# Softcap attention and a maxout layer on one core: the handwritten order of the work rearranged from the second pair of heads to about the tenth quad

## The chip, the cores and the metric

The kernel runs on one core of a Trainium2 chip. The core has four engines that compute, each with its own queue of instructions: TensorE (PE in the profile, with its weight loads as PEld) multiplies matrices into PSUM, VectorE (DVE) works element by element, ScalarE (ACT) evaluates functions, and GpSimd (POOL) here mostly issues loads. SyncE (SP) issues the other transfers and passes on some waits. The metric is the device time of one execution in microseconds (us), as the median of several runs.

## The reference

Attention with a soft cap over 8 batches, 12 heads, 448 tokens and 64 columns a head; its output, 3,584 rows of 768, goes through a maxout layer of width 1,024. Inputs and output are float32.

```python
scores = scale * np.matmul(q, k.transpose(0, 1, 3, 2))      # scale = 1/sqrt(64)
scores = cap * np.tanh(scores / cap)                         # cap = 30
attn = np.exp(scores - max); attn = attn / (sum(attn) + 1e-09)
x = np.matmul(attn, v)           # heads side by side: 3584 x 768
h1 = x @ w1; h2 = x @ w2         # 768 x 1024
out = np.maximum(h1, h2) @ w_out # 1024 x 768
```

## The kernel before, in words

**What is computed.** max(x w1, x w2) w_out is written as relu(x wd) w_out + x wm, with wd = w1 - w2 and wm = w2 w_out. Both are made in the kernel at its start (steps W and WC turn w2 around, P with OP and PC multiply it by w_out, `sub` subtracts). Work is in bf16, sums in float32. Softmax takes no maximum, since tanh bounds the scores.

**How it is tiled.** Two heads are a pair (i = 0 to 47), two pairs a quad (t = 0 to 23). For each pair, TensorE makes scores transposed (keys on the partitions) in three blocks of 128 keys, steps `S i 0` to `S i 2`; the last 64 keys of a quad's four heads are one more block, step `L t`, the left scores. ACT takes each block through tanh (`T i j`, and `TL t`) and then exp over one to three blocks (`E i j0 j1`, `EL t`). DVE adds the blocks up (`A`, `B`; from quad 3 on), TensorE totals them (`Y t`), DVE inverts the totals (`Y1`, `Y2`, `Y3`), TensorE multiplies with the values (`VL t`, `V t u j0 j1`), and DVE normalizes (`N t 0` one instruction, L613; `N t 1` two, L616) into xT, the transposed x.

The maxout layer is 120 groups, 15 on average a batch: a group is one PSUM bank of 128 rows, summed over 6 blocks (448 columns, relu(x wd), kept transposed as gT) or over 14 blocks (384 columns, half an output tile: 6 of x wm and 8 of gT w_out). `O g bank` opens it. `M x y n` makes n steps in which the upper 64 rows of the array work for group x and the lower 64 for group y, side by side; x = y uses all 128 rows. So a group's two halves are made one after the other, by different rows of the array, into one bank. Between the halves stands a hand-over, `H g` on DVE or `Hs g` on SyncE: an instruction that computes nothing, waits for the last matmul of one half, and is waited for by the first of the other (L647 to L650). `ev g` takes a finished group out of PSUM on DVE (L661 with relu, L697 as a copy), `eva g` on ACT (L695).

**PSUM.** Two score slots s0 and s1 of two banks each are shared by S, L and the values: block j of pair i takes the slot `TURN[o*3+j] ^ (t%2)` with TURN = (0,1,0,1,1,0) and o the pair's place in the quad. The left scores take the slot that `s_tile(1, t)` names, the values that of `s_tile(0, t+1)`. So the third scores of the second pair of a quad, `S i 2` with odd i, take the slot that the values of the quad before were in, and cannot begin before that quad's normalize is done. Four banks mm0 to mm3 serve all else: groups, totals, transposes, premultiplication.

**Loads and turns.** GpSimd's queue loads q, k (lq, lk) and v (lv) with a cast to bf16, and the weights (lw1, lw2, lwo). The first five quads are turned by TensorE (X, copied by DVE with XC); from quad 5 on SyncE's queue issues a transposing transfer (`cr t`, L470), which waits for that quad's loads. SyncE also issues the output's stores (st).

**What sets the order.** One long text, ORDER, lines 9 to 195, names every step in turn, and a loop at the end runs it through a table of steps. The schedule is manual: on each engine the instructions stand in the order of the text, and waits come from the data, the buffers and the hand-overs alone. `D bank n` are dummy matmuls near the start. The changed text is found by step names; the profile shows lines:

- L411 W, L426 P, L432 PC, L453 X, L458 XC, L466 D
- L509 S, L514 T, L523 L, L527 TL, L531 E, L534 EL, L543 A, L548 B
- L561, L565, L568 Y, L573 Y1, L576 Y2, L579 Y3, L595 VL, L601 V, L613 and L616 N
- L640 M by halves, L635 M by whole rows, L661, L695, L697 evacuations

Of the kernel before, what the change touches and what calls it, by code (L numbers as in the profile page):

```python
# [14 lines left out]
OP 2 0 3; P 2 0 7; P 1 0 1; P 2 0 1; P 1 0 1; P 3 0 2; P 1 0 2; PC 2 0; PC 1 0; E 1 2 3; E 1 0 2; TL 1; T 2 0; EL 0;
S 3 0; S 2 2; P 3 0 1; W 0 2; P 3 0 1; X 4 3; T 2 2; T 3 0; VL 0; Y 0 1; V 0 0 0 3; V 0 1 0 3; S 3 1; lwo 1 0;
lwo 1 1; lq 5 0; lk 5 0; lv 1 0; lv 1 1; lk 8 0; lq 8 0; lq 7 0; lw2 4; lv 6 2; lq 6 0; lk 7 0; lk 6 0; lw2 5; lw1 2;
lw1 4; lw1 0; lv 2 0; lv 2 1; WC 0; PC 3 0; XC 4; Y1 0; Y2 0; Y3 0; N 0 0; N 0 1; E 2 0 3; T 3 1; EL 1; E 3 0 2;
OP 0 0 1; P 0 0 2; OP 2 1 2; P 2 1 2; P 0 0 1; OP 1 1 3; P 1 1 2; P 0 0 1; P 1 1 2; P 0 0 1; P 1 1 4; S 4 0; S 3 2;
X 5 0; P 2 1 4; P 0 0 3; P 2 1 1; XC 5; PC 1 1; PC 0 0; T 3 2; T 4 0; E 3 2 3; OP 3 1 3; P 3 1 1; P 2 1 1; S 4 1;  # L20
S 4 2; Y 1 1; T 4 1; T 4 2; L 2; P 3 1 4; VL 1; TL 2; V 1 1 0 3; V 1 0 0 3; S 5 0; X 6 0; E 4 0 3; T 5 0; EL 2; Y1 1;
Y2 1; PC 2 1; Y3 1; N 1 1; N 1 0; XC 6; X 7 2; W 4 1; S 5 2; S 5 1; X 8 0; P 3 1 3; WC 4; XC 8; PC 3 1; T 5 1; T 5 2;
OP 4 0 1; P 4 0 2; OP 0 1 0; P 0 1 3; S 6 0; S 6 1; W 5 3; P 0 1 1; P 4 0 6; P 0 1 4; E 5 0 2; T 6 1; T 6 0; E 5 2 3;
XC 7; sub 2 0; WC 5; sub 4 0; PC 4 0; sub 0 0; PC 0 1; OP 5 1 3; P 5 1 4; S 6 2; L 3; Y 2 1; T 6 2; TL 3; E 6 0 3;
VL 2; V 2 1 0 1; V 2 0 0 3; V 2 1 1 3; S 7 0; P 5 1 4; OP 5 0 0; P 5 0 8; Y1 2; Y2 2; Y3 2; N 2 0; N 2 1; A 3 0 1;
A 3 0 2; PC 5 1; PC 5 0; T 7 0; EL 3; lk 9 0; lq 11 0; lv 3 1; lq 9 0; lw1 1; lw1 3; lq 10 0; lk 12 1; lv 3 0; lw1 5;
lk 10 0; lk 11 0; lk 11 1; lk 10 1; S 7 2; O 0 1; M 0 -1 2; S 7 1; M 0 -1 4; O 1 2; M 1 -1 1; T 7 2; T 7 1; Hs 0;
M 1 -1 1; S 8 1; M 1 -1 1; M 1 0 3; S 8 0; X 9 3; OP 4 1 0; P 4 1 4; sub 1 0; sub 3 0; XC 9; T 8 1; E 7 0 2; T 8 0;
E 7 2 3; P 4 1 4; L 4; O 2 3; M 2 0 3; S 8 2; M 2 1 3; A 3 1 1; B 3 1; PC 4 1; ev 0; B 3 0; Hs 2; TL 4; T 8 2; O 3 0;
# [12 lines left out]
VL 5; A 5 1 2; TL 6; V 5 0 0 2; V 5 1 0 2; Y 5 3; E 12 0 3; V 5 0 2 3; V 5 1 2 3; Y1 5; S 13 0; M 13 11 1; lv 7 0;
M 13 11 1; Y2 5; M 13 12 2; Y3 5; M 13 12 1; lv 7 1; M 13 12 3; N 5 0; M 13 12 1; lv 7 2; M 13 12 1; T 13 0;
M 13 12 1; N 5 1; M 13 12 1; lv 7 3; M 13 12 1; O 14 3; M 14 12 2; EL 6; Hs 13; S 13 1; lk 18 0; M 14 12 1;
M 14 13 1; ev 11; M 14 13 1; Hs 12 2; T 13 1; S 13 2; lk 18 1; M 14 13 1; A 6 0 1; M 12 13 2; T 13 2; Hs 14;
M 12 13 1; lq 18 0; A 6 0 2; S 14 0; M 12 13 3; E 13 0 2; M 12 13 1; S 14 1; lk 19 0; M 12 13 1; O 15 0; M 15 13 2;
ev 12; M 15 13 1; lk 19 1; M 15 14 2; ev 13; M 15 14 1; T 14 0; O 16 1; M 16 14 1; lq 19 0; A 6 1 1; M 16 14 1;
st 0 1; M 16 14 1; Hs 15; T 14 1; cr 8; B 6 0; M 16 15 1; S 14 2; M 16 15 1; ev 14; M 16 15 1; T 14 2; O 17 2;
M 17 15 2; H 16; M 17 15 1; B 6 1; M 17 16 2; E 13 2 3; M 17 16 1; ev 15; O 18 3; M 18 16 1; L 7; VL 6; A 6 1 2;
st 0 2; TL 7; V 6 0 0 2; V 6 1 0 2; Y 6 0; E 14 0 3; V 6 0 2 3; V 6 1 2 3; Y1 6; S 15 0; M 18 16 1; lv 8 0;  # L50
M 18 16 1; Y2 6; M 18 17 1; Y3 6; M 18 17 1; lv 8 1; M 18 17 1; O 19 0; M 19 17 2; ev 16; Hs 18; lv 8 2; M 19 17 1;
M 19 18 1; T 15 0; N 6 0; M 19 18 2; lv 8 3; O 20 1; M 20 18 2; EL 7; Hs 19; ev 17; M 20 18 1; lk 20 0; S 15 1;
M 20 19 1; N 6 1; M 20 19 1; T 15 1; M 20 19 1; lk 20 1; O 21 2; M 21 19 3; Hs 20; M 21 20 1; lq 20 0; ev 18;
# [147 lines left out]
def kernel(  # L201
# [17 lines left out]
    B, H, S, D = q.shape  # L219
# [554 lines left out]
```

## Time and profile before

| | before |
|---|---|
| runs | 328.42, 327.58, 328.32 us; median 328.32 |
| profiled execution | 328.19 us, span 326.4 us |
| TensorE busy | 319.9 us, 98% of the span |
| ScalarE busy | 281.0 us, 86% |
| VectorE busy | 240.2 us, 74% |
| GpSimd busy | 161.8 us, 50% |
| TensorE's granted clock | 1.00 |
| moved by DMA | 46.28 MB, mean 142 GB/s |

The profiled execution is one run: its time contains its span and 1.8 us around it. A row of the timeline gives start and length, engine, line, operation, output and inputs, and how many instructions it groups; brackets at its end hold the engine's idle time before it and what ended that. A row of a grouping gives the count, the busy time, the mean in ns, and idle time before with what released it. TensorE's ends are modelled, so two of its rows may overlap, and the distance of two starts says more than a length.

### The profile page before, as it was taken

Reading aid. Unit: us, or ns where it says so; the run is one execution under the profiler, and the core shown is the slowest. Engines: PE = TensorE matmul, PEld = TensorE weight load, DVE = VectorE, ACT = ScalarE, POOL = GpSimd, SP = SyncE. Lnnn points to the kernel's source line nnn. Section 1 sums busy time; section 2 is a strip of 40 time slices with the busy share of each in tenths; the row PEclk is TensorE's granted clock in tenths of the full one; section 3 lists DMA queues with packets and bytes.
Section 4 is the critical chain, followed back from the end, with each engine's and each line's share of the span. In section 5 each row is a group of like instructions: output and inputs, shape, how many; then the busy total and the mean of one; then the engine's idle time right before and its main releaser. Section 6 shows DMA issues by size and latency. Waiting matters only on the chain.

```text
span 326.4 us, 9772 instructions
## 1 busy us (share of the span) xinstructions
PE 319.9 (98%) x4138; PEld 183.6 (56%) x4138; DVE 240.2 (74%) x422; ACT 281.0 (86%) x278; POOL 161.8 (50%) x237
## 2 busy tenths in 40 slices
PE   7999999999999999999999999999999999999994
PEld 3454545545656664565565565556466555557662
DVE  3346899987897778987897788968878779773201
ACT  5999999999999999999999999999999999921120
POOL 7357583677764682665775475578538311000000
PEclk9999999999999999999999999999999999999999
DMA  8999999899999999999999999999999963013033
GB/s 181 180 201 178 273 252 115 95 141 140 189 183 109 142 189 184 97 89 181 167 181 113 202 106 189 121 166 163 184 109 90 212 157 44 2 50 98 0 98 96
DMA packets 134507, 46.28 MB, mean 142 GB/s; under 512 B 112320, under 2 KB 129472, under 8 KB 134464
## 3 DMA queue, kind: packets, MB, share of 16 engines
q0 software_dynamic: 94592, 25.02, 77.6%
q1 hardware_dynamic: 39424, 19.99, 29.9%
q8 instruction: 32, 0.52, 0.7%
q10 hardware_dynamic: 448, 0.66, 0.6%
q14 instruction: 11, 0.09, 0.1%
HBM read 47.78 MB, written 11.01 MB: 180 GB/s over the span
## 4 chain that ended last, share of the span: by engine, by line
PE 94%; DMA 2%; DVE 1%; POOL 1%; issue 0%
PE mm L640 61%; PE s L509 9%; PE s L601 9%; PE mm L426 5%; DMA w2b<-in_moe_w_dram 2%; PE s L523 2%; PE mm L568 2%; PE s L595 2%; PE mm L635 1%; POOL kqs L316 1%; PE mm L453 1%; PE mm L411 1%; PE mm L561 1%; DVE xT L616 0%; PE mm L466 0%; DVE xT L613 0%
## 5 line engine op out<-in xcount | busy, mean ns | idle before, releaser
L514 ACT ACTIVATE e<-s 128x896 bf16<-128x896 f32 x144 | 125.7, 926 | 5.5 <-PE s L509 5.0
L531 ACT ACTIVATE e<-e 128x1792 bf16<-128x1792 bf16 (+2 forms) x72 | 122.8, 1708 | 0.0
L640 PE MATMUL mm<-wo_sb,gT 64*128 64x384 bf16 x864 | 115.2, 323 | 0.0
L640 PE MATMUL mm<-wm_sb,xT 64*128 64x384 bf16 x648 | 102.1, 322 | 0.0
L640 PE MATMUL mm<-xT,wd_sb 64*128 64x448 bf16 x768 | 97.6, 349 | 0.0
L323 POOL DMA_DIRECT2D kqs<-in_k_dram x76 | 54.6, 720 | 55.1 <-DMA qkT<-kqs 50.9
L640 PEld LDWEIGHTS <-gT 64*128 64x128 bf16 x864 | 58.6, 94 | 25.6 <-issue 1.1
L640 PEld LDWEIGHTS <-wd_sb 64*128 64x128 bf16 x768 | 48.3, 94 | 27.1 <-issue 2.1
L640 PEld LDWEIGHTS <-xT 64*128 64x128 bf16 x648 | 50.1, 94 | 18.5 <-issue 0.2
L509 PE MATMUL s<-qkT 64*128 64x448 bf16 x288 | 52.5, 352 | 0.2 <-DVE xT L613 0.2
L347 POOL DMA_DIRECT2D vp<-in_v_dram x48 | 30.4, 637 | 37.4 <-PE s L509 25.4
L661 DVE TENSOR_SCALAR gT<-mm 128x448 bf16<-128x448 f32 x64 | 39.0, 618 | 8.4 <-PE mm L640 7.6
L323 POOL DMA_DIRECT2D kqs<-in_q_dram x38 | 35.0, 922 | 3.9 <-issue 1.8
L601 PE MATMUL s<-e,vp 128*32 128x448 bf16 x576 | 36.1, 354 | 0.0
L543 DVE TENSOR_TENSOR esum<-e 128x896 bf16<-128x896 bf16 x42 | 25.9, 618 | 9.1 <-ACT e L531 9.1
L616 DVE TENSOR_TENSOR xT<-s,inv 64x448 bf16<-64x448 f32 x48 | 29.8, 622 | 1.7 <-PE s L601 0.8
L543 DVE TENSOR_TENSOR esum<-esum,e 128x896 bf16<-128x896 bf16 x42 | 26.2, 624 | 5.9 <-ACT e L531 4.8
L509 PEld LDWEIGHTS <-qkT 64*128 64x128 bf16 x288 | 18.7, 94 | 20.1 <-issue 11.3
L695 ACT COPY osb<-mm 128x384 f32<-128x384 f32 x10 | 4.8, 479 | 26.9 <-PE mm L640 26.7
L697 DVE COPY osb<-mm 128x384 f32<-128x384 f32 x44 | 23.3, 554 | 6.2 <-PE mm L640 5.7
L548 DVE TENSOR_TENSOR esum<-esum,el 64x896 bf16<-64x896 bf16 x42 | 26.0, 619 | 1.2
L573 DVE STREAM_TRANSPOSE st<-mm 128x448 f32<-128x448 f32 x24 | 15.6, 649 | 12.9 <-PE mm L568 11.3
(57 smaller groups left out, 269.9 us busy)
## 6 DMA issues: line engine op xcount, KB each, us to landing
out_dram<-osb SPq DMA_DIRECT2D x54, 192.0 KB, 4.8
vp<-in_v_dram POOLq DMA_DIRECT2D x38, 160.0 KB, 3.9
kqs<-in_q_dram POOLq DMA_DIRECT2D x46, 112.0 KB, 5.3
kqs<-in_k_dram POOLq DMA_DIRECT2D x76, 56.0 KB, 3.9
osb<-in_moe_w_dram POOLq DMA_DIRECT2D x4, 512.0 KB, 6.9
w2b<-in_moe_w_dram POOLq DMA_DIRECT2D x6, 256.0 KB, 7.7
wo_sb<-in_moe_w_out_dram POOLq DMA_DIRECT2D x4, 384.0 KB, 9.9
vp<-in_v_dram POOLq DMA_DIRECT2D x10, 128.0 KB, 7.8
```

The costliest lines, as they stand in the source:

```text
L323: nc.gpsimd.dma_start(out=to, in_=x)
L347: nc.gpsimd.dma_start(out=to, in_=x)
L509: scored[i, j] = nc.tensor.matmul(s[:, h, :S], k_of(t, o, h, j), q_of(t, o, h)).ins
L514: nc.scalar.activation(expo[i][:, 2 * j : 2 * j + 2, :], slots[i, j][:, :, :S], AF.Tanh, scale=scale / cap)
L531: nc.scalar.activation(e, e, AF.Exp, scale=float(cap))
L543: nc.vector.tensor_add(d, e[:, 0:2, :] if j == 1 else d, e[:, 2 * j : 2 * j + 2, :])
L548: nc.vector.tensor_add(d, d, left_e[t][r, :, :])
L601: nc.tensor.matmul(vals[t][place(m, u), u, :S], w[:, m, :], expo[2 * t + o][:, 2 * j + h, :], start=False, stop=(j == NJ - 1))
L616: nc.vector.tensor_mul(x[64 - r : 128 - r], vals[t][r : r + 64, u, :S], sums[t, 3][64 - r : 128 - r])
L640: ins = nc.tensor.matmul(self.ps, w[r], x[r], start=first, stop=self.at == [self.n, self.n]).ins
L661: nc.vector.tensor_relu(gT[b // 2][:, f, cs], ps)
L697: nc.vector.tensor_copy(o[:, hs], ps)
```

## The change

ORDER is another text from the second pair on. Each kind of step occurs as often as before. Loads, DMA issues and hand-overs are also at other places of the text, but the order on each queue is what counts:

- GpSimd's queue: no difference.
- TensorE: another order from about 12.6 us of the profile before to the step S 20 2, which begins at 122.39; all later steps are in the same order.
- ACT: another order from quad 1 to E 19 2 3 (pair 19). The evacuations of groups 24, 27 and 29 move from DVE to ACT.
- DVE: another order up to about quad 10.
- SyncE: another order up to about the transfer of quad 13.
- Hand-overs on DVE 31 in place of 21, on SyncE 103 in place of 107; the groups 1, 10, 12, 17, 24 and 27 have one at a place where there was none.
- Some steps use another of the four banks (W, X, Y, P, and groups 26 and 27).

One line of code differs, in the transposes: the bank is taken when one is named, and not when the part is other than 1. For the steps of this text the two give the same. The text is five lines longer, so L640 of before is L645 of after.

```diff
-T 1 0; T 1 2; lw2 1; lwo 0 0; lwo 0 1; lw2 0; lq 4 0; lk 4 0; lv 0 0; lv 0 1; XC 3; XC 2; WC 3; D 0 4; S 1 1; D 0 8;
-D 2 2; S 2 1; W 1 2; WC 2; WC 1; T 1 1; T 2 1; S 2 0; D 0 4; L 1; OP 3 0 0; P 3 0 2; OP 1 0 1; P 1 0 4; P 3 0 2;
...
-S 4 2; Y 1 1; T 4 1; T 4 2; L 2; P 3 1 4; VL 1; TL 2; V 1 1 0 3; V 1 0 0 3; S 5 0; X 6 0; E 4 0 3; T 5 0; EL 2; Y1 1;
-Y2 1; PC 2 1; Y3 1; N 1 1; N 1 0; XC 6; X 7 2; W 4 1; S 5 2; S 5 1; X 8 0; P 3 1 3; WC 4; XC 8; PC 3 1; T 5 1; T 5 2;
...
-M 20 19 1; N 6 1; M 20 19 1; T 15 1; M 20 19 1; lk 20 1; O 21 2; M 21 19 3; Hs 20; M 21 20 1; lq 20 0; ev 18;
-M 21 20 1; S 15 2; S 16 0; ev 19; M 21 20 1; T 15 2; O 22 3; M 22 20 1; lk 21 0; M 22 20 1; A 7 0 1; Hs 21;
...
+W 2 1; WC 3; T 1 2; lv 1 0; S 1 1; WC 2; D 3 4; lv 1 1; D 2 4; T 1 1; S 2 1; D 2 8; T 2 1; S 2 0; W 1 0; T 2 0; L 1;
+WC 1; E 1 2 3; S 2 2; OP 3 0 2; P 3 0 1; OP 2 0 0; P 2 0 2; TL 1; OP 1 0 3; P 1 0 1; P 2 0 1; P 3 0 1; P 1 0 2; EL 0;
...
+P 0 0 1; Y2 1; VL 1; PC 0 0; V 1 0 0 3; E 4 0 3; Y3 1; V 1 1 0 3; S 5 0; N 1 1; X 7 1; X 6 0; lq 11 0; P 3 1 1;
+T 5 0; P 3 1 1; N 1 0; P 3 1 2; W 4 2; lv 3 1; EL 2; XC 6; S 5 1; lq 9 0; WC 4; S 5 2; T 5 1; X 8 0; lw1 1; XC 7;
...
+M 18 16 1; Y1 6; M 18 16 2; M 18 17 1; lv 8 1; M 18 17 1; Y2 6; S 15 0; ev 16; M 18 17 1; lv 8 2; O 19 0; M 19 17 2;
+Hs 18; st 0 2; Y3 6; M 19 17 1; T 15 0; lv 8 3; M 19 18 3; ev 17; O 20 1; M 20 18 1; EL 7; M 20 18 1; S 15 1; H 19;
+N 6 1; M 20 18 1; M 20 19 1; T 15 1; M 20 19 2; O 21 2; M 21 19 3; H 20; ev 18; E 15 0 2; M 21 20 2; lk 20 0;
+M 21 20 1; N 6 0; S 16 0; O 22 3; M 22 20 2; lk 20 1; H 21; ev 19; S 15 2; M 22 20 1; M 22 21 1; T 16 0; cr 9;
...
+E 17 0 2; Hs 26; st 1 3; M 24 25 1; lk 23 1; M 24 25 4; lq 23 0; M 24 25 2; O 27 3; M 27 25 2; eva 24; M 27 25 1;
...
 """
...
     def transposes(i, bank, c=None):
 
-        if c != 1:
+        if bank is not None:
             turned["qk", i] = mm_tile(bank).bitcast(bf16)
         ps = turned["qk", i]
```

More of the change, by code (lines that the diff above doesn't have):

```diff
@@ L15 @@
[L15 to L19, printed above, removed]
@@ L25 @@
[L25 to L29, printed above, removed]
@@ new lines @@
+Y3 4; M 10 9 1; lv 6 1; M 10 9 1; M 8 9 1; EL 5; M 8 9 1; Hs 10; S 11 1; N 4 0; lk 14 1; M 8 9 3; T 11 1; N 4 1;
+M 8 9 2; lq 14 0; M 8 9 1; O 11 0; M 11 9 2; E 11 0 2; M 11 9 1; M 11 10 1; lv 5 1; M 11 10 1; ev 8; M 11 10 3;
+A 5 0 1; S 11 2; M 11 10 3; T 11 2; A 5 0 2; M 11 10 1; lq 16 0; S 12 0; M 11 10 1; ev 9; M 11 10 1; O 12 1;
+M 12 10 1; T 12 0; M 12 10 1; H 11; A 5 1 1; S 12 1; lv 6 3; M 12 10 1; M 12 11 1; T 12 1; M 12 11 1; Hs 10; B 5 0;
+lv 6 0; M 12 11 1; S 12 2; M 10 11 2; B 5 1; T 12 2; lk 16 1; M 10 11 1; cr 7; M 10 11 4; lk 17 0; E 11 2 3;
@@ new lines @@
+T 19 0; N 8 1; M 26 27 2; lv 10 3; M 26 27 3; EL 9; M 26 27 1; lk 24 1; Hs 28; M 26 27 1; S 19 1; N 8 0; O 29 2;
+M 29 27 2; T 19 1; lq 24 0; M 29 27 1; M 29 28 1; ev 26; M 29 28 1; S 19 2; M 29 28 1; A 9 0 1; eva 27; M 29 28 1;
+lk 25 0; cr 11; M 29 28 1; S 20 0; T 19 2; A 9 0 2; M 29 28 2; lk 25 1; M 29 28 3; T 20 0; M 29 28 1; lq 25 0;
+S 20 1; O 30 3; M 30 28 2; E 19 0 2; M 30 28 1; S 20 2; Hs 29; M 30 29 1; Hs 28; M 30 29 2; M 28 29 4; T 20 2;
+M 28 29 1; A 9 1 1; M 28 29 3; H 30; O 31 0; M 31 29 1; T 20 1; M 31 29 1; ev 28; M 31 29 1; M 31 30 1; B 9 1;
@@ new lines @@
+A 14 1 2; TL 15; V 14 0 0 2; V 14 1 0 2; E 30 0 3; Y 14 0; V 14 0 2 3; V 14 1 2 3; Y1 14; S 31 0; M 58 56 1;
+M 58 57 1; Y2 14; M 58 57 1; Hs 56; M 58 57 1; Y3 14; M 56 57 2; Hs 58; M 56 57 1; lk 36 0; M 56 57 1; N 14 0;
+M 56 57 2; T 31 0; M 56 57 1; lv 16 0; M 56 57 1; N 14 1; O 59 0; M 59 57 2; EL 15; M 59 57 1; lv 16 1; M 59 58 1;
+S 31 1; M 59 58 2; lv 16 2; T 31 1; M 59 58 1; ev 56; S 31 2; M 59 58 1; ev 57; M 59 58 1; lv 16 3; M 59 58 1;
+T 31 2; M 59 58 1; A 15 0 1; S 32 0; lk 36 1; M 59 58 3; E 31 0 2; A 15 0 2; O 60 3; M 60 58 1; lq 36 0; S 32 1;
@@ new lines @@
+lv 18 2; S 36 0; ev 68; M 71 69 2; M 71 70 1; lv 18 3; E 35 0 2; M 71 70 1; ev 69; S 36 1; M 71 70 2; lk 40 1;
+M 71 70 3; st 4 0; M 71 70 1; lq 40 0; M 71 70 2; T 36 0; M 71 70 1; A 17 1 1; O 72 0; M 72 70 3; lk 41 0; H 71;
+T 36 1; B 17 0; M 72 71 1; S 36 2; M 72 71 2; lk 41 1; H 70; B 17 1; M 70 71 1; T 36 2; M 70 71 3; lq 41 0;
+M 70 71 2; E 35 2 3; M 70 71 2; O 73 1; M 73 71 1; ev 70; L 18; VL 17; A 17 1 2; TL 18; V 17 0 0 2; V 17 1 0 2;
+E 36 0 3; Y 17 3; V 17 0 2 3; V 17 1 2 3; Y1 17; S 37 0; lk 42 0; M 73 71 2; Y2 17; M 73 72 2; Y3 17; M 73 72 1;
@@ new lines @@
+E 40 0 3; Y 19 1; V 19 0 2 3; V 19 1 2 3; Y1 19; lk 46 0; S 41 0; M 82 83 2; Y2 19; lv 21 0; M 82 83 2; Y3 19;
+M 82 83 2; lv 21 1; M 82 83 1; O 85 1; M 85 83 1; N 19 0; M 85 83 2; T 41 0; lv 21 2; M 85 84 2; N 19 1; M 85 84 2;
+lv 21 3; EL 20; M 85 84 2; S 41 1; M 85 84 1; lk 46 1; M 85 84 1; T 41 1; M 85 84 1; ev 82; S 41 2; M 85 84 1;
+lq 46 0; ev 83; M 85 84 1; O 86 3; M 86 84 1; T 41 2; M 86 84 1; Hs 85; A 20 0 1; S 42 0; M 86 84 1; M 86 85 1;
+lk 47 0; M 86 85 1; E 41 0 2; A 20 0 2; Hs 84; M 86 85 1; S 42 1; M 84 85 1; Hs 86; lk 47 1; cr 22; M 84 85 4;
@@ new lines @@
+lq 47 0; M 84 85 3; T 42 0; O 87 2; M 87 85 1; A 20 1 1; M 87 85 2; M 87 86 1; ev 84; T 42 1; M 87 86 2; S 42 2;
+st 5 3; ev 85; M 87 86 2; T 42 2; M 87 86 1; B 20 0; M 87 86 4; B 20 1; E 41 2 3; M 87 86 1; st 5 4; O 88 0;
+M 88 86 2; L 21; VL 20; A 20 1 2; TL 21; V 20 0 0 2; V 20 1 0 2; E 42 0 3; Y 20 1; V 20 0 2 3; V 20 1 2 3; Y1 20;
+S 43 0; lv 22 0; M 88 86 1; M 88 87 1; Y2 20; M 88 87 1; Hs 86; M 88 87 1; Y3 20; lv 22 1; M 86 87 2; Hs 88;
+M 86 87 2; N 20 0; lv 22 2; M 86 87 2; T 43 0; M 86 87 2; N 20 1; lv 22 3; O 89 1; M 89 87 2; EL 21; M 89 87 1;
@@ new lines @@
+M 104 102 2; Hs 103; M 104 102 1; M 104 103 2; Hs 102; M 104 103 1; M 102 103 2; Hs 104; st 6 1; M 102 103 6;
+O 105 0; M 105 103 2; eva 102; M 105 103 1; M 105 104 2; eva 103; M 105 104 1; O 106 1; M 106 104 2; Hs 105;
+M 106 104 1; M 106 105 2; ev 104; M 106 105 1; O 107 2; M 107 105 2; Hs 106; M 107 105 1; M 107 106 2; ev 105;
+M 107 106 1; O 108 3; M 108 106 2; Hs 107; st 6 2; M 108 106 1; M 108 107 2; ev 106; M 108 107 1; O 109 0;
+M 109 107 2; H 108; M 109 107 1; M 109 108 2; ev 107; M 109 108 1; O 110 1; M 110 108 2; Hs 109; M 110 108 1;
@@ new lines @@
+M 110 109 2; ev 108; M 110 109 1; O 111 2; M 111 109 2; Hs 110; M 111 109 1; M 111 110 2; ev 109; M 111 110 1;
+O 112 3; M 112 110 2; Hs 111; M 112 110 1; M 112 111 2; ev 110; M 112 111 1; O 113 0; M 113 111 2; Hs 112;
+M 113 111 1; M 113 112 2; ev 111; M 113 112 9; O 114 1; M 114 112 2; Hs 113; M 114 112 1; M 114 113 2; Hs 112;
+M 114 113 1; M 112 113 2; Hs 114; M 112 113 6; O 115 2; M 115 113 2; eva 112; M 115 113 1; M 115 114 2; eva 113;
+M 115 114 3; st 7 3; M 115 114 6; O 116 3; M 116 114 2; Hs 115; M 116 114 1; M 116 115 2; Hs 114; M 116 115 1;
@@ L197 @@
+M 114 115 2; Hs 116; M 114 115 6; O 117 0; M 117 115 2; eva 114; M 117 115 1; M 117 116 2; eva 115; M 117 116 3;
+st 7 4; M 117 116 6; M -1 116 2; Hs 117; M -1 116 1; M -1 117 2; Hs 116; M -1 117 1; M 116 117 8; M -1 117 2;
+eva 116; M -1 117 1; O 118 1; M 118 118 1; eva 117; M 118 118 4; st 7 5; M 118 118 9; O 119 2; M 119 119 2; ev 118;
+M 119 119 12; ev 119; st 7 6;
 """
```

310 lines of the change are left out of this document (139 added, 171 removed).

## The prediction

> **What bounds the kernel now.** I read the page first, then busy time by stage, then single rows.
>
> ```profile
> PE 319.9 (98%) x4138; PEld 183.6 (56%) x4138; DVE 240.2 (74%) x422; ACT 281.0 (86%) x278; POOL 161.8 (50%) x237
> PE 94%; DMA 2%; DVE 1%; POOL 1%; issue 0%
> 34.40:62.30 27.90, 27.74 (x386) 14.58 (x385) 27.25 (x43) 27.90 (x28) 15.22 (x22) 1.00 1.21 198
> 73.00:125.00 52.00, 52.00 (x694) 31.46 (x688) 42.63 (x76) 50.68 (x51) 33.50 (x47) 1.00 1.39 156
> ```
>
> TensorE (PE) is 98% busy and is 94% of the chain of waits. From 34.4 to 62.3 us DVE (27.25 of 27.90) and ACT (all of it) are full as well, so all three bound that stage; later ACT is at 50.68 of 52.00 and DVE has room (columns: stretch, its length, PE, weight load, DVE, ACT, POOL, clock, DMA share, GB/s). The clock is 1.00, so time can only come from waits or from work. A busy PE is a model, so a short wait hides in it: I look at spacings, not at durations.
>
> **How much TensorE loses before the orders meet again.** The two orders have the same TensorE steps up to the step behind the one at 122.39 (S 20 2), and from there the same order. Their ends of that part, and the spacings of undisturbed units:
>
> ```profile
> 6.53 0.55 PE L509 MATMUL s<-qkT 64*128 64x448 bf16 x4
> 46.97 0.81 PE L426 MATMUL mm<-wo_sb,w2T 128*128 128x384 bf16 x4
> 47.73 0.36 PE L509 MATMUL s<-qkT 64*128 64x448 bf16 x2
> 94.31 1.68 PE L640 MATMUL mm<-xT,wd_sb 64*128 64x448 bf16 x16
> 95.82 0.54 PE L509 MATMUL s<-qkT 64*128 64x448 bf16 x4
> 100.09 0.32 PE L640 MATMUL mm<-wm_sb,xT 64*128 64x384 bf16 x1
> 100.58 0.32 PE L640 MATMUL mm<-wm_sb,xT 64*128 64x384 bf16 x1
> 122.39 0.49 PE L509 MATMUL s<-qkT 64*128 64x448 bf16 x2
> 124.52 0.38 PE L523 MATMUL s<-qkT 64*32 64x448 bf16 x8
> ```
>
> ```profile
> L640 PE MATMUL mm<-wo_sb,gT 64*128 64x384 bf16 x221 | 29.9, 323 | 0.0
> L640 PE MATMUL mm<-wm_sb,xT 64*128 64x384 bf16 x168 | 26.9, 323 | 0.0
> L640 PE MATMUL mm<-xT,wd_sb 64*128 64x448 bf16 x198 | 26.7, 349 | 0.0
> L509 PE MATMUL s<-qkT 64*128 64x448 bf16 x126 | 23.0, 353 | 0.2 <-DVE xT L613 0.2
> L426 PE MATMUL mm<-wo_sb,w2T 128*128 128x384 bf16 x96 | 17.3, 327 | 0.0
> L601 PE MATMUL s<-e,vp 128*32 128x448 bf16 x216 | 13.3, 354 | 0.0
> ```
>
> Three pairs of 384 columns take 100.58 - 100.09 = 0.49 us, 0.163 each; eight pairs of 448 take 95.82 - 94.31 = 1.51 us, 0.189 each. Four full-height matmuls from 46.97 should end 4 x 0.163 = 0.65 later; the half-height scores start 0.76 later: a change of tile size costs 0.11, which I round to 0.1. I count with 0.160 and 0.187, a little under both. The second fence groups that part by shape (count, busy): halves run two at a time and values four, so its six rows are 389/2 x 0.160 + 198/2 x 0.187 + 126/2 x 0.187 + 96 x 0.160 + 216/4 x 0.187 = 86.9 us; transposes, left scores, totals and dummies priced alike, and 54 size changes, bring the count of all steps from 6.53 to S 20 2 to 112.4. They took 122.39 - 6.53 = 115.9, so 3.5 us are lost. Where a unit begins later than its predecessor allows:
>
> ```profile
> 13.18 0.62 PE L411 MATMUL mm<-ident,w2b 128*128 128x128 bf16 x8 [0.41 <-DMA w2b<-in_moe_w_dram]
> 35.58 0.62 PE L411 MATMUL mm<-ident,w2b 128*128 128x128 bf16 x8
> 36.36 0.55 PE L509 MATMUL s<-qkT 64*128 64x448 bf16 x4 [0.16 <-DVE xT L613]
> 35.68 0.62 DVE L613 TENSOR_TENSOR xT<-s,inv 128x448 bf16<-128x448 f32 x1
> 67.47 0.68 PE L568 MATMUL mm<-esum,ones 128*32 128x448 bf16 x4
> 67.80 0.55 PE L601 MATMUL s<-e,vp 128*32 128x448 bf16 x4
> 85.94 1.48 PE L640 MATMUL mm<-xT,wd_sb 64*128 64x448 bf16 x13
> 87.33 0.37 PE L509 MATMUL s<-qkT 64*128 64x448 bf16 x2
> 101.07 0.48 PE L640 MATMUL mm<-wm_sb,xT 64*128 64x384 bf16 x2
> 101.49 0.38 PE L523 MATMUL s<-qkT 64*32 64x448 bf16 x8
> ACT e L514 <- PE s L509: 1.9, 3, 1.0
> 96.22 0.92 ACT L514 ACTIVATE e<-s 128x896 bf16<-128x896 f32 x1 [0.73 <-PE s L509]
> ```
>
> First, 0.5 us at 13 us: the second load of w2. Second, waits on other engines, 1.6 in all: eight of 0.12 to 0.28 us, near 30.7, 36.2 (the scores at 36.36 need the score slot that the normalize at 35.68 reads until 36.30), 48.1, 50.4, 64.5, 67.8 (totals at 67.47: four column groups side by side should be past after 0.19, the next starts after 0.33), 87.0 (13 halves from 85.94 need 1.22, the next row begins after 1.39), 101.1 (one pair and a size change need 0.26, and it took 0.42), and smaller ones. The rest, 3.5 - 0.5 - 1.6 = 1.4, is a steady 0.012 us per us by which units are slower than my prices. ACT is pulled along: it waited for scores 1.9 us in three waits (0.73 of it at 96.22).
>
> **The change, part by part.**
> - *Same work.* Each kind of step has its count of before; the code edit in the transposes issues nothing else. POOL's queue is the same 233 steps, so a load moves only where a buffer comes free at another time. This costs 0.
> - *TensorE's order, about 13 to 122 us.* The w2 wait stays: the load that it waits for is the same. Tile-size changes go from 54 to 57: 3 x 0.1 = **+0.3**. The drift of 1.4 stays. The neighbours of the eight waits are others now, so **-1.6**; in their place I walked the new order with the spacings above and the durations of the producers' rows. The scores S 2 2 come about **0.15** too early for the tanh that frees their slot (T 2 0); elsewhere the producer is done first, by 0 to 0.7 us. The tightest cover is the normalize ahead of the third scores of each odd pair: 0 to 0.3 us at seven of them (S 7 2 to S 19 2). If all seven lost what the scores at 36.36 lost (0.16), that is 1.1 us; if none did, 0. I take **0.05**, near none, because before was as tight at 62.48 (below) and lost nothing to speak of there.
> - *ACT.* Three evacuations (groups 24, 27, 29) move from DVE to ACT:
>
> ```profile
> L695 ACT COPY osb<-mm 128x384 f32<-128x384 f32 x10 | 4.8, 479 | 26.9 <-PE mm L640 26.7
> 34.41 1.26 DVE L616 TENSOR_TENSOR xT<-s,inv 64x448 bf16<-64x448 f32 x2 [0.85 <-PE s L601]
> 61.02 1.26 DVE L616 TENSOR_TENSOR xT<-s,inv 64x448 bf16<-64x448 f32 x2
> 62.31 0.62 DVE L661 TENSOR_SCALAR gT<-mm 128x448 bf16<-128x448 f32 x1
> 62.48 0.35 PE L509 MATMUL s<-qkT 64*128 64x448 bf16 x2
> DVE osb L697 <- PE mm L640: 2.5, 3, 1.0
> ```
>
>   3 x 0.479 = 1.44 us more on ACT behind 100 us. Its steps at their spacing then reach T 20 2 at 119.6; before it began that tanh when the scores at 122.39 had come, near 122.9, so about 3.3 us of cover hide the 1.44. Without that cover it costs all of 1.44.
> - *DVE.* The full stretch starts where the values of quad 1 end (the 0.85 us wait at 34.41). In the new order fewer premultiply units stand ahead of them, so it starts about 0.45 us sooner, with the same work; the normalize that let S 9 2 go at 62.48 (61.02 + 1.26 = 62.28) ends near 61.9, where TensorE now wants it at 61.9. That keeps the cover, no more: 0.
> - *Hand-overs.* Ten more stand on DVE instead of SyncE (21 to 31), and some groups that had one on SyncE or none shift. A hand-over is a wait for the last matmul of one half of a bank, not counted as busy; on DVE everything behind it (additions, inversions, normalize) waits too, and TensorE's third scores wait for normalize. The trace times none. Bounds: 0 if the half is past when DVE gets there, at most the longest wait of DVE on such a matmul, 1.0 us (row L697 above). By my walk only those of groups 7, 20 and 30 come within 0.2 us of their time. I take **0.05** in all, near the lower end, and the upper end is rival 1.
> - *Transfers.* The quads' transposes wait for loads, and those for buffers:
>
> ```profile
> 87.02 2.19 SPq L470 DMA_TRANSPOSE qkT<-kqs  x1
> DMA to landing us min/median/max: 4.2/6.3/9.5
> ```
>
>   The one for quad 8 would be issued near 86.9 (87.02 now). Its first scores are wanted about 94.7; they ran at 95.9 to 96.0 (the second half of the four matmuls from 95.82). With 4.2 / 6.3 / 9.5 us to landing that is 3.6 early, 1.5 early, or 1.7 late. I take **0** and keep 1.7 as a bound; in this trace it took nearer 8, which is just in time. On SyncE's queue a transpose issue stands for 2.19 us (the row's second column) ahead of any hand-over behind it; by the walk the nearest, that of group 24 behind quad 10's, still has 0.2 us: 0.
>
> Sum: -1.6 + 0.3 + 0.15 + 0.05 + 0.05 = **-1.05 us**. The left scores at 124.52 then come at about 123.5, and the 204 us behind them, in the same order on TensorE, follow. The profiled execution took 328.19 us (span 326.4 and 1.8 around it), 0.13 under the median of the three runs (328.32): 328.19 - 1.05 = 327.1, and at the median's level 327.3; I say **327.2 us**.
>
> The Trainium skill, "TensorEngine Tiling (Array Packing)", section Key Properties, speaks against the change: changing the tiling mode drains TensorE. The trace agrees that a change costs (0.11 at 47.73). It states no price; were a drain a whole matmul of 0.35 us instead, three more would be 1.05 and the sum -0.3.
>
> **Rivals.**
> 1. *Hand-overs hold DVE (slower).* If TensorE's halves end later than the walk says when DVE reaches a hand-over, DVE stands still with normalize queued behind, the third scores come late, and the tanh of ACT behind them, once in each of the quads 4 to 9. DVE's three waits on such matmuls last 2.5 / 3 = 0.83 us; if half of one reaches TensorE, that is 0.4 a quad, 6 x 0.4 = 2.5, and -1.05 + 2.5 = +1.45: **329.7**. For it: DVE at 27.25 of 27.90, and covers near nothing. Against it: behind 73 us DVE has 18% free (42.63 of 52.00). It decides from 0.25 us a quad, where the gain is gone.
> 2. *The next transfer sets the pace (no change).* Being ahead, TensorE meets quad 8's transpose: a landing 0.8 late of the range above returns 0.8 of the 1.05: **328.0**. For it: a landing of about 8 us in this trace; against: the median of 6.3.
> 3. *ACT becomes the bound.* If the scores still reach ACT with its 1.9 us of waits, the 1.44 are not covered and nothing is won: 328.2 + 1.4 = **329.6**. Against it: the 3.3 us of room.
> 4. *The order changes nothing.* Eight other waits of the same size stand where these were; only the tile-size changes count, +0.3: **328.5**. For it: the covers that are left are as thin as the old ones were. Against it: the walk of before with the same prices showed its waits where the trace has them.
>
> Rival 1 needs DVE to work strictly in order; the Trainium skill, "TensorE: Matmul & The Clock Gate" (engine queue depths), says so of VectorE's queue, and no row here can show it for hand-overs, since they leave none.
>
> **How the numbers follow.** About 0.3% (1.0 us) is what a measurement of this kernel can tell from no change: faster is below 327.3, slower above 329.3. Forecast 0.48, with its own range 326.5 (no price of the sum but the drift and half the tile changes) to 328.0 (five of the seven normalizes lose 0.16); rival 1 0.25, rival 2 0.10, rival 3 0.05, rival 4 0.12. Faster: most of the forecast, whose lower half and centre lie there, and the part of rivals 2 and 4 in which little comes back: 0.42. Slower: rival 3 and nearly all of rival 1: 0.29. Same: the rest, 0.29. The range runs from 326.3 (a little under the forecast's own) to 329.9, just past rivals 1 and 3, since they are too likely to be left out.
>
> **What would show it.** Right: the step at 122.39 comes at about 121.3, the scores at 36.36 and 95.82 show no gap before them, ACT's wait for scores falls below 1.2 us, all later rows are 1 us earlier. Wrong: DVE idle with nothing named before a normalize between 62 and 120 us (rival 1); PE waiting for the quad-8 transpose (2); ACT at 52 of 52 us behind 73 (3); third scores late at other quads by 0.15 each (4). The forecast fails if the common step comes later than 122.0.

## The result, and the profile after

| | before | after |
|---|---|---|
| median of 22 runs | 328.19 us | 328.83 us |
| lowest to highest | 327.58 to 328.76 us | 327.23 to 332.35 us |
| profiled execution, span | 328.19, 326.4 us | 328.74, 327.0 us |

The changed kernel is slower: ratio 1.0028, 95% interval 1.0017 to 1.0039. That is 0.6 us by the medians and 0.9 by the ratio, where 1.05 us less was forecast. The ratios leave out runs over 1.5% above the fastest of their kernel (here the one of 332.35 us), so they are not the quotients of the medians. The second row says as much as the first: its best run beats the best of before by 0.35 us, and its runs reach over 5.1 us where those of before reach over 1.2.

From the page of the changed kernel (busy time, and the chain of waits), then its busy time by stage (columns as before: stretch, length, PE, weight load, DVE, ACT, ...):

```profile
PE 319.4 (98%) x4138; PEld 183.3 (56%) x4138; DVE 239.0 (73%) x419; ACT 282.0 (86%) x281; POOL 161.7 (49%) x237
PE 91%; DMA 4%; ACT 3%; issue 0%; DVE 0%; SPq 0%
```

```profile
34.40:62.30 27.90, 27.27 (x368) 14.37 (x362) 26.59 (x43) 27.10 (x27) 15.17 (x21) 1.00 1.10 187
73.00:125.00 52.00, 51.55 (x680) 30.27 (x682) 40.73 (x72) 51.69 (x53) 34.93 (x49) 1.00 1.52 164
125.00:289.00 164.00, 164.00 (x2155) 94.71 (x2154) 136.46 (x240) 157.31 (x152) 83.19 (x118) 1.00 1.14 136
```

TensorE now has holes: 0.63 us from 34.40 to 62.30 us (0.16 before), 0.45 from 73 to 125 us (none before). In the chain TensorE's share fell from 94 to 91%, and DMA's rose from 2 to 4%. Three rows of its timeline with what ended the idle time before them (the second is the first scores of quad 7; L654 is the hand-over), and the step that the forecast used as a mark:

```profile
35.60 0.25 PE L458 MATMUL mm<-ident,kqs 64*64 64x64 bf16 x4 [0.63 <-issue]
...
85.41 0.36 PE L514 MATMUL s<-qkT 64*128 64x448 bf16 x2 [0.23 <-DMA qkT<-kqs]
...
109.22 0.33 PE L645 MATMUL mm<-wo_sb,gT 64*128 64x384 bf16 x1 [0.21 <-SPq L654]
...
124.96 0.39 PE L528 MATMUL s<-qkT 64*32 64x448 bf16 x8
```

The mark, the left scores of quad 10, comes at 124.96; before it was 124.52, and 123.5 was forecast. By the prediction's count of spacings the three rows stand for 0.79, 0.42 and 0.38 us, 1.59 together. Without them the mark would be at 123.37. So in this execution the order without them would be as quick as forecast, and three waits that the forecast put at nothing take more than the gain. Behind quad 11 the two profiles run 0.53 us apart to the end, step by step.

### The profile page after: what moved, and what is told of

Same layout as the page of the kernel before. It is cut to its first block, busy times and chain, and to the rows that moved or that the text cites. A ratio compares the mean times of both kernels' runs of the same rounds, so it can differ in the third digit from the quotient of the medians.

```text
span 327.0 us, 9782 instructions
## 1 busy us (share of the span) xinstructions
PE 319.4 (98%) x4138; PEld 183.3 (56%) x4138; DVE 239.0 (73%) x419; ACT 282.0 (86%) x281; POOL 161.7 (49%) x237
## 4 chain that ended last, share of the span: by engine, by line
PE 91%; DMA 4%; ACT 3%; issue 0%; DVE 0%; SPq 0%
PE mm L645 59%; PE s L514 9%; PE s L606 9%; PE mm L431 5%; DMA qkT<-kqs 3%; PE s L528 2%; ACT e L519 2%; PE mm L573 2%; PE s L600 2%; PE mm L640 1%; PE mm L458 1%; DMA kr<-in_k_dram 1%; ACT e L536 1%; PE mm L566 1%; PE mm L416 0%
## 5 line engine op out<-in xcount | busy, mean ns | idle before, releaser
L536 ACT ACTIVATE e<-e 128x2688 bf16<-128x2688 bf16 (+2 forms) x72 | 123.0, 1713 | 0.1
L645 PE MATMUL mm<-wo_sb,gT 64*128 64x384 bf16 x864 | 115.2, 323 | 0.2 <-SPq L654 0.2
L645 PE MATMUL mm<-wm_sb,xT 64*128 64x384 bf16 x648 | 102.9, 323 | 0.0
L645 PE MATMUL mm<-xT,wd_sb 64*128 64x448 bf16 x768 | 98.3, 349 | 0.0
L645 PEld LDWEIGHTS <-gT 64*128 64x128 bf16 x864 | 58.1, 94 | 27.1 <-issue 1.5
L645 PEld LDWEIGHTS <-wd_sb 64*128 64x128 bf16 x768 | 49.0, 94 | 26.6 <-issue 2.1
L645 PEld LDWEIGHTS <-xT 64*128 64x128 bf16 x648 | 50.0, 94 | 19.1 <-issue 0.7
L352 POOL DMA_DIRECT2D vp<-in_v_dram x48 | 30.4, 638 | 36.7 <-PE s L514 22.9
L606 PE MATMUL s<-e,vp 128*32 128x448 bf16 x576 | 35.1, 354 | 0.0
L700 ACT COPY osb<-mm 128x384 f32<-128x384 f32 x13 | 6.2, 479 | 27.1 <-PE mm L645 26.9
L702 DVE COPY osb<-mm 128x384 f32<-128x384 f32 x41 | 22.0, 554 | 5.4 <-PE mm L645 4.7
```

Of the source, the lines that this page charges most:

```text
L352: nc.gpsimd.dma_start(out=to, in_=x)
L536: nc.scalar.activation(e, e, AF.Exp, scale=float(cap))
L606: nc.tensor.matmul(vals[t][place(m, u), u, :S], w[:, m, :], expo[2 * t + o][:, 2 * j + h, :], start=False, stop=(j == NJ - 1))
L645: ins = nc.tensor.matmul(self.ps, w[r], x[r], start=first, stop=self.at == [self.n, self.n]).ins
L702: nc.vector.tensor_copy(o[:, hs], ps)
```

## The experiments

All of them are the new or the old text with steps moved. Medians, extremes and ratios, each against before on the same chip:

| | median us | lowest to highest | ratio, interval |
|---|---|---|---|
| x1 early only | 327.95 | 327.08 to 328.96 | 0.9994, 0.9984 to 1.0003 |
| x2 late only | 329.38 | 328.03 to 330.70 | 1.0039, 1.0021 to 1.0056 |
| x3 hand-over of 24 first | 330.89 | 327.73 to 333.66 | 1.0048, 1.0014 to 1.0081 |
| x4 quad 7's loads first | 328.73 | 327.46 to 336.68 | 1.0019, 1.0002 to 1.0036 |
| x5 three hand-overs to DVE | 329.16 | 328.05 to 333.24 | 1.0036, 1.0015 to 1.0056 |
| x6 before, one behind a transpose | 329.44 | 329.08 to 329.81 | 1.0046, 1.0033 to 1.0060 |
| x7 13 hand-overs back | 331.19 | 330.65 to 334.94 | 1.0122, 1.0085 to 1.0159 |
| x8 x5, and quad 7's transpose | 327.98 | 327.14 to 329.11 | 0.9999, 0.9988 to 1.0011 |
| x9 12 more weight loads and matmuls | 328.87 | 327.28 to 332.16, and one of 546.54 | 1.0041, 1.0015 to 1.0067 |
| x10 quad 8's transpose before a store | 328.22 | 327.27 to 331.95 | 1.0008, 0.9986 to 1.0029 |
| x11 all three | 327.92 | 327.23 to 330.39 | 1.0001, 0.9983 to 1.0018 |
| x12 x11 without the hand-overs | 328.02 | 327.13 to 331.37 | 1.0009, 0.9988 to 1.0030 |
| x13 x2 repaired | 327.95 | 327.67 to 328.47 | 0.9986, 0.9975 to 0.9998 |
| x14 old start, new rest, repaired | 327.26 | 326.94 to 328.18 | 0.9966, 0.9954 to 0.9978 |
| x15 6 more weight loads and matmuls | 327.58 | one run | |
| x16 18 more weight loads and matmuls | 330.21 | one run | |

Each kernel has one profiled execution as well. This is what TensorE lost in it at three places, read as jumps of its steps against the count of spacings (us; the first near 35.6, the second at the first scores of quad 8, the third at hand-overs behind a transposing transfer):

| | start | quad 8 | hand-overs |
|---|---|---|---|
| before, x2, x6, x13, x14 (old start) | 0 in all | 0 in all | x6 1.41, x2 0.16 |
| after | 0.79 | 0 | 0.38 |
| x1, x11 | 0.1, 0 | 0 | 0 |
| x3, x4 | 0.77, 0.40 | 0, 0 | x3 none at 24, 0.28 at 26; x4 none above 0.12 |
| x5, x7, x8 | 0, 1.9, 0.4 | 1.69, 1.11, 1.01 | x7 1.03 and 0.42 |
| x10, x12 | 2.5, 0.3 | 0, 0 | 0.42, 0.37 |
| x9, x15, x16 | 0, 0.2, 0 | 0, 0, 1.35 | x16 0.75 |

The first scores of quad 7 waited in the changed kernel's profile alone (0.42).

**Which part loses.** The new order to the left scores of quad 6 and the old one behind (x1, whose seam is shown), and the reverse (x2):

```diff
 M 13 11 1; ev 10;
-L 6; lk 16 0; VL 5; H 12; TL 6; A 5 1 2; V 5 1 0 2; V 5 0 0 2;
+L 6; VL 5; A 5 1 2; TL 6; lk 16 0; lk 17 1; lq 17 0; st 0 0; V 5 0 0 2; V 5 1 0 2;
...
```

> The new order up to the left scores of quad 6 (about 78 us), the old one from there on. Theory A (the new order is quicker by itself, but its covers over the transposing transfers and over their issue on SyncE are thin, and that costs about 0.4 us each at quads 7 and 10): no later transfer is late here, so 0.3 to 1 us faster than before (the profiled run was 0.35 ahead at that point), with a spread like that of before. Theory B (hand-overs on DVE): only a few of them are left, so the same. Theory C (the early order itself loses, by the 0.63 us that TensorE stood in the transposes at 35.6): 0 to 0.5 us slower than before.

> The old order up to the left scores of quad 6, the new one from there on. Theory A: slower than before by 0.5 to 1.2 us, with TensorE waiting for the transpose of quad 7 or 8 or for the hand-over of group 24, and a wide spread. Theory B: slower by the same amount, but with DVE standing still at hand-overs and TensorE waiting for normalize. Theory C: within 0.3 us of before.

x1 is 0.2 us below before (327.95 against 328.15), its interval reaching both sides of 1; x2 is 1.2 us above (329.38). The late part loses, and the early part does not give its gain in every run.

**Single repairs in the new order.** x3 and x4:

```diff
-A 8 0 1; cr 10; T 17 2;
+A 8 0 1; T 17 2;
...
-Hs 24; T 18 1;
+Hs 24; cr 10; T 18 1;
```

```diff
-lk 14 0; lv 6 1; lk 14 1; lq 14 0; lv 5 1;
+lk 14 0; lk 14 1; lq 14 0; lv 6 1; lv 5 1;
```

> The new order with one step moved: on SyncE the transpose issue of quad 10 stands behind the hand-over of group 24 in place of ahead of it. Theory A: the 0.38 us before the step at 109.2 are gone, so 0.2 to 0.4 us faster than the changed kernel. Theories B and C: the same as the changed kernel.

> The new order with one load moved: on GpSimd's queue the load of v for quad 6 that waits for a buffer stands behind the last load of q for quad 7. Theory A: the transpose of quad 7 is issued 1 to 2.5 us sooner (74 to 75 us), its first scores no longer wait (0.42 us in the profiled run), the time falls by 0.3 to 0.5 us against the changed kernel and its spread narrows. Theories B and C: the same as the changed kernel.

Neither did what was expected. x3 freed the hand-over of group 24 (no jump there), but now that of group 26 stands behind the same transpose and starts 0.11 us after its issue ends, and half of its runs are above 332 us, of which its profiled run (328.63) was none. Five of these six have a mean granted clock of 0.994 or 0.995 (see the last section), so its median says little of the edit. In x4 the transpose of quad 7 was issued at 76.0, as in the changed kernel (76.2): its loads were there, but on SyncE's queue a hand-over of group 10, which passes at about 76, stands ahead of it. That led to x8.

**Where hand-overs stand.** x5 puts three on DVE, x6 puts one of the old order behind a transpose, x7 undoes the move to DVE, x8 repairs quad 7 on top of x5. x5, in the new order:

```diff
-Hs 17;
+H 17;
...
-Hs 24;
+H 24;
...
-Hs 26;
+H 26;
```

x6, in the kernel before, where `cr 8` stands ahead of it:

```diff
-H 16;
+Hs 16;
```

x7, with 13 lines of this kind; x8 has those of x5, the load of x4, and the second hand-over of group 10:

```diff
-H 7;
+Hs 7;
...
-Hs 10;
+H 10;
```

> The new order; three hand-overs that stand behind a transposing transfer on SyncE's queue (group 17 behind that of quad 8, groups 24 and 26 behind that of quad 10) are put on DVE. Theory A, made narrower (TensorE waits for SyncE, which stands at the issue of a transpose that itself waits for loads and takes 1.3 to 3.3 us): TensorE no longer starts 0.11 us after the end of such an issue, the time falls by 0.5 to 1.2 us against the changed kernel, to 327.6 to 328.3, and the highest runs go. Theory B (hand-overs on DVE hold normalize): slower than the changed kernel by 0.2 to 0.6.

> The order before, with one hand-over moved from DVE to SyncE, that of group 16, which there stands behind the transpose of quad 8 (issued 87.0 to 89.2 us, while TensorE wants the second half near 88.5). Theory A: TensorE starts that half 0.11 us after the issue's end, so 0.5 to 1 us slower than before, and a wider spread. Theory B: the same as before or a little faster.

> The new order, with the 13 hand-overs of groups 7 to 30 that it has on DVE and the old one on SyncE put back on SyncE. Theory A: no faster than the changed kernel, and slower by 0.5 or more where one of them now stands behind a transpose (groups 9, 12, 14, 22). Theory B: faster than the changed kernel by 0.5 to 1.5 us.

> As x5, and also what holds the transpose of quad 7: the hand-over of group 10 ahead of it on SyncE goes to DVE, and the load of v for quad 6 stands behind the last load of q for quad 7. Theory A: that transpose is issued 1 to 2.5 us sooner (from 76.2), its scores wait in no run, 0.2 to 0.5 us faster than x5. Theory B: slower than x5.

x6, its timelines of TensorE and of SyncE:

```profile
89.71 0.74 PE L645 MATMUL mm<-xT,wd_sb 64*128 64x448 bf16 x6 [1.23 <-SPq L654]
```

```profile
86.68 2.92 SPq L475 DMA_TRANSPOSE qkT<-kqs  x1
```

One hand-over moved costs 1.4 us in the kernel before (329.44 against 328.04): the issue holds SyncE until 86.68 + 2.92 = 89.60, and TensorE goes on 0.11 us later. x7 bears on the first rival: with 13 hand-overs taken off DVE the kernel is 331.19, 1.2% above before in place of 0.3%. By itself this does not show that they stood well on DVE, since some now stand behind a transpose (1.03 and 0.42 us in its profile). x14 below does: with 35 hand-overs on DVE, against 21 before, it is faster than before. But x5 is no better than the changed kernel. Its profile has the reason (TensorE):

```profile
96.43 0.36 PE L514 MATMUL s<-qkT 64*128 64x448 bf16 x2 [1.52 <-DMA qkT<-kqs]
```

The first scores of quad 8 waited for the landing of its transpose. That is one more cause, of the same size. x8 is level with before, so it gains about 0.7 us on the changed kernel (quad 7's transpose is now issued at 74.2); its profiled run (329.11) was its slowest, with 1.01 us lost at quad 8 again.

**Quad 8's transpose, and the stall near 35.6.** x10, in the new order:

```diff
-Hs 15; lq 18 0; st 0 1;
+Hs 15; lq 18 0;
...
-H 16; cr 8; B 6 0;
+H 16; cr 8; st 0 1; B 6 0;
```

x11 is x8 with this edit, x12 the same without the three hand-overs of x5. x9 cuts dummy matmuls (16 steps of one in place of one of 16); x15 does so with `D 1 8`, x16 with both:

```diff
-D 1 16;
+D 1 1; D 1 1; D 1 1; D 1 1;
...
```

> The new order, with one run of 4 dummy matmuls of 512 columns near 9 us cut into 16 of 128 columns: the same columns, 12 weight loads and 12 matmuls more on TensorE's queue. If TensorE's stall near 35.6 us, which no row names, is a wait for its own instructions (a 16 KB packet of the instruction queue begins 2.3 to 2.4 us before the stall ends, and the stalled transpose is the 53rd of 56 in every run that had it), the stalled one is now the 41st, 12 earlier, or, if that packet lands sooner, there is no stall at all. If it is a wait for data, a bank or the quad's loads, it stays at the 53rd. Time: within 0.6 us of the changed kernel.

> The new order with one step moved on SyncE's queue: the transposing transfer of quad 8 ahead of the store of the second output tile, which stood ahead of it. Theory A, in its last form (the loads of quad 8 and with them its transpose come later than before, its first scores sooner, and TensorE waits for the landing: 0 in the profiled run of the changed kernel, 1.0 to 1.7 in those of x5, x7 and x8): issue near 87.1 in place of 88.3, landing about 1 us sooner, and the time falls by 0.3 to 0.8 us against the changed kernel. Theory B': what costs is the place of hand-overs alone: the same as the changed kernel.

> x8 with the move of x10 as well: no hand-over behind the transposes of quads 8 and 10, quad 7's and quad 8's transposes issued sooner. Theory A: scores of quads 7 and 8 wait 0 to 0.5 us at most, so 327.2 to 327.7, faster than both kernels by 0.1 to 0.3% of before. Theory B': the same as x8.

> x11 without the three hand-overs put on DVE (groups 17, 24 and 26 are on SyncE again, behind the transposes). Theory A: slower than x11 by 0.2 to 0.6 us (the 0.38 of the step at 109.2, and group 17 when the transpose of quad 8 is issued late). If hand-overs behind transposes do not matter in this order, the same as x11.

x10 gains 0.6 us on the changed kernel by its median. x11 is not below x8, and against x12 it is 0.1 better, which is within the noise. None of x8, x10, x11 and x12 is clear of before. x9 (median 328.87) had no stall in its profiled run (327.28 us), so it told nothing of the cause; that run is of use below. x10's profiled run was its worst, 331.95 us, and shows the stall at its largest. Its TensorE timeline, and its busy time by stretch:

```profile
37.75 0.32 PE L458 MATMUL mm<-ident,kqs 64*64 64x64 bf16 x4 [2.30 <-issue]
38.00 1.46 PE L431 MATMUL mm<-wo_sb,w2T 128*128 128x384 bf16 x4
```

```profile
35.30:38.00 2.70, 0.40 (x15) 0.26 (x9) 0.86 (x2) 1.80 (x3) 1.59 (x2) 0.93 1.00 381
38.00:42.00 4.00, 4.00 (x52) 2.31 (x50) 2.08 (x4) 1.16 (x2) 1.29 (x2) 0.62 1.48 205
```

TensorE stands 2.3 us, and then four microseconds follow at a mean granted clock of 0.62 (0.50 up to 41.00 us, 0.99 in the last of them): four matmuls take 1.25 us to the next row where the row at 46.97 before had 0.76. That is 2.5 + 1.4 us lost in one place.

**The two open causes.** x13, in x2 (24 and 26 as 17):

```diff
-Hs 15; lq 18 0; st 0 1;
+Hs 15; lq 18 0;
...
-H 16; cr 8; B 6 0;
+H 16; cr 8; st 0 1; B 6 0;
...
-Hs 17;
+H 17;
...
```

x14 is before up to `L 3`, then the text of x11; one bank is another at the seam:

```diff
-Y 2 3;
+Y 2 1;
```

> x2 (the old order up to the left scores of quad 6, the new one behind) with two of the repairs of x11: the transpose of quad 8 ahead of the store on SyncE, and the hand-overs of groups 17, 24 and 26 on DVE. In x2 nothing stood near 35 us, and yet it lost 1.2 us to before. Theory A: that loss is the late landing of quad 8's transpose and the hand-overs behind transposes, so at least 0.8 us faster than x2, 327.8 to 328.5. If something else in the late order loses: 329 or more, as x2.

> The old order up to the left scores of quad 3 (42.6 us), the new one from there with the three repairs of x11. Theory A with the stall near 35.6 as a second cause that belongs to the new start: no stall there, 327.3 to 327.9, and no run above 329.5 (those of x11 reach 330.4, of x10 332.0). If the stall is not bound to the new start: the same spread as x11.

> The new order with 6 weight loads and 6 matmuls more ahead of 9 us (2 dummy matmuls of 512 columns cut into 8 of 128). If the stall is a wait for instructions, it stands, where it shows, ahead of the transpose 6 places earlier than in the changed kernel (the 47th in place of the 53rd of 56); if for data, ahead of the 53rd. Time: as the changed kernel.

> As x15 with 18 weight loads and 18 matmuls more: a wait for instructions stands ahead of the 35th transpose, a wait for data ahead of the 53rd. Time: as the changed kernel.

x13 takes back all that x2 lost: 329.38 to 327.95, and the highest run from 330.70 to 328.47. x14 is 0.34% faster than before (0.9966, interval 0.9954 to 0.9978), with no run above 328.18; it beats both kernels. Behind 24 us its profile names one wait of TensorE:

```profile
PE s L514 <- DVE xT L618: 0.2, 1, 0.2
```

So the stall belongs to the new start, and the rest of the loss to quad 8's transpose and the hand-overs behind transposes. x13 mends these two together, and how the loss divides between them is not shown: by time x10 alone gains 0.6 us, x5 alone nothing. x15 had a small stall, and at the place told; TensorE's timeline cut in two there, and the DMA view of 32.7 to 32.9 us:

```profile
34.12 0.91 PE L458 MATMUL mm<-ident,kqs 64*64 64x64 bf16 x46
...
35.03 0.34 PE L458 MATMUL mm<-ident,kqs 64*64 64x64 bf16 x10
```

```profile
q8 instruction: 1, 0.02, 30.5%
```

The hole of 0.2 us (the model lets the rows overlap it) lies after 46 transposes, where the changed kernel's lies after 52: six pairs of instructions more ahead, six transposes sooner. A wait for data would have stayed. And one packet of the instruction queue begins at 32.8, 2.2 us before TensorE goes on; in the changed kernel it is 33.17 and 35.60, in x10 35.37 and 37.75, both 2.4. It is a wait for TensorE's own instructions. The profiles without a stall fit: with the new start TensorE comes to that place 2.2 to 2.3 us after the packet begins in x1 and x11 (holes of 0.09 and 0.03), and 2.6 to 4.6 us after it in x5, x9 and x16. x16 (330.21 us) had none, so its 35th place could not be seen; it shows the other two waits instead:

```profile
91.93 0.55 PE L645 MATMUL mm<-xT,wd_sb 64*128 64x448 bf16 x3 [0.58 <-SPq L654]
...
97.45 0.36 PE L514 MATMUL s<-qkT 64*128 64x448 bf16 x2 [0.99 <-DMA qkT<-kqs]
```

## Why the prediction was wrong

- **The count of TensorE's order: right.** x9's profiled run, the fastest of its eight, is the new order with no stall. Its mark, and its stage from 73 us on:

```profile
123.50 0.38 PE L528 MATMUL s<-qkT 64*32 64x448 bf16 x8
```

```profile
73.00:125.00 52.00, 52.00 (x698) 30.91 (x692) 40.98 (x73) 51.78 (x55) 34.19 (x48) 1.00 1.46 164
```

  The mark was forecast at 123.5, and the run's 327.28 us as 327.2. That it fits so closely is in part luck: two terms were off in opposite directions, since the w2 wait of 0.5 did not stay, and S 2 2 waited 0.4 in place of 0.15.
- **ACT: right.** The 1.44 us were hidden in x9. But ACT is now at 51.78 of 52.00 us there, which suggests, though no run shows it, that the next gain in that stretch is not to be had from TensorE's order alone.
- **Normalize and hand-overs on DVE: right,** and the first rival, the likeliest of them, was wrong (x14; x9, too, shows no wait of TensorE for normalize from 17 us on).
- **"Transfers: I take 0": this step failed.** In the changed kernel's profile it was quad 7's transpose, which the prediction does not price, that was late: issued at 76.21, landed at 85.37, 0.42 us lost. Quad 8's cost nothing there, because the two waits ahead (0.79 + 0.42) had put TensorE 1.2 us later (96.04, against 94.80 in x9), and the landing at 95.99 was just in time. In four other profiles it cost 1.0 to 1.7, as far as the prediction's bound of 1.7. I put its issue at 86.9; it came at 88.28. The loads ahead of it are later. GpSimd's timeline, before and then after:

```profile
68.65 0.64 POOL L347 DMA_DIRECT2D vp<-in_v_dram  x1 [1.65 <-PE s L601]
```

```profile
70.58 0.64 POOL L352 DMA_DIRECT2D vp<-in_v_dram  x1 [3.78 <-PE s L606]
```

  The load of v for quad 6 waits until the values of quad 4 are done, now 1.9 us later, and all loads behind it on the queue move with it (those of quad 8 by 1.4, the last landing 2.5 us later, at 86.46). That alone did not set the issue: the hand-over of group 15, ahead of it on SyncE's queue, passes at 86.75, where it passed at 86.69 before. What set it is a store: before, it stands ahead of that hand-over, and the transpose follows the hand-over by 0.33 us; now it stands between the two, and the transpose follows by 1.53. Before (the second of the store's two issues, and the hand-over and the transpose come after it):

```profile
84.52 0.59 SPq L676 DMA_DIRECT2D out_dram<-osb  x1
```

  and after:

```profile
86.88 1.11 SPq L681 DMA_DIRECT2D out_dram<-osb  x2
88.28 3.27 SPq L475 DMA_TRANSPOSE qkT<-kqs  x1
```

  In x9 all the loads are in at 83.75, and the issue still follows the hand-over by 1.54; in x13, with the store moved behind, by 0.33. And TensorE wants that quad 1.2 us sooner (94.80 in x9, where the landing at 93.86 was in time, against 96.01 before). From issue to landing it took 6.0 to 9.2 us in the ten profiles with the new late order and the store ahead, and 5.0 to 6.6 in the five with the store behind; 6.5 to 7.7 were left to it (94.80 less the issues at 88.28 and, in x9, at 87.10). The median of 6.3, taken over all transposes of before, was too short for this one.
- **"That of group 24 ... still has 0.2 us: 0": failed.** The issue took 2.56 us (106.55 to 109.11, and TensorE's row at 109.22) where the prediction names 2.19, quad 8's of before; the row of all issues before (ns, lowest, median, highest) had the warning:

```profile
L470 SPq DMA_TRANSPOSE qkT<-kqs x19: 1301/1598/2663, 55.1 to 262.2; - x19
```

  It cost 0.38. The cover was mis-sized too: issues of 2.34, 2.55, 2.56 and 2.60 us cost 0.16 (x2), 0.37 (x12), 0.38 (the changed kernel) and 0.42 (x10), so everything above 2.18 is lost, and at 2.19 nothing was left, and not 0.2. The hand-over of group 17, new and behind quad 8's transpose, was not priced at all: it starts 0.11 us after the issue's end in the changed kernel, and costs 0.75 in x16.
- **The wait for instructions was in no term.** It is the largest single loss of the profiled run, 0.79. With the 0.42 and 0.38 above it makes up the 1.6 us between the forecast (1.05 less) and this execution (0.55 more).
- **The rivals.** The second (quad 8's transpose sets the pace) was one of the three causes, in other runs than the profiled one, with too small a price, since it was taken alone, and a chance of 0.10. The time lies in the range; the sign was wrong.

## What to carry to other kernels

When an order is tightened, what it waited for was also what covered transfers that vary from run to run: price a transfer by its slowest landing and its issue by its longest, and not by the median, wherever less than that is left. An instruction that only passes a wait on must not stand on a queue behind one that itself waits for loads; look there first when a kernel's runs spread. Judge such a change by its lowest run and its spread as well as by the median: here they told that the order was good and that its covers, and the instructions near its start, were not.

## What the hardware showed that was not expected

TensorE can wait for its own instructions in the middle of a kernel: 0.2 to 2.5 us in eight of the thirteen profiles with the new start, in none of the five with the old. In seven of the eight a packet of the instruction queue begins 2.2 to 2.4 us before TensorE goes on (in x12 3.5, where the packet itself took 2.8 us in place of 0.9 to 1.0). With the old start it begins at 30.4 to 31.1 us, with the new one at 31.8 to 35.4 in all but x9 and x16 (30.4 and 30.5, no stall). The Trainium skill, "Runtime: NRT & Kernel Launch", section Instruction fetch mechanics, says that instructions come in blocks of 16 KiB over the engine's own DMA queue and that the cost of a block is mostly hidden. The packets here have that size; hidden they are with the old start and not with the new. Why the packet comes later there stays open: nothing was moved to test it.

After the hole of 2.3 us the granted clock fell, to a mean of 0.62 over four microseconds (x10). The Trainium skill, "TensorE: Matmul & The Clock Gate", Part 1, puts the drop behind about 3.4 us without work; here 2.7 us with hardly any were enough. In x7 TensorE stood at the same place for less, and its clock stayed at 1.00:

```profile
36.69 0.25 PE L458 MATMUL mm<-ident,kqs 64*64 64x64 bf16 x4 [1.75 <-issue]
```

That the other runs above 331 us of kernels with the new start have the same cause is argued and not shown. Four microseconds at 0.62 take about 0.005 off a run's mean clock (an estimate from x10's row), and 11 of these 15 runs have a mean of 0.990 to 0.995, as x10's has 0.995, while no run with the old start is below 0.997. The other four, two of them x7's, have 0.999 or 1.000 and need another cause. The run of 546.54 us in x9, with a mean clock of 0.56, is not among the 15 and stays unexplained.
